# A gated recurrence in front of a routed expert layer: 29 instead of 24 warm-up products at the start of TensorE's queue

## The chip, the cores and the metric

The kernel runs on one core of one Trainium2 chip. The time is the device time of one execution in microseconds (us); the time of a kernel is the median of several executions. Lower is better.

## The reference

The first half is a recurrence over 768 tokens for 4 batches and 8 heads of width 48. Its output, 3072 rows of 384, goes to a layer of eight experts, where each row uses the one expert that its gate favours:

```python
f = 1.0 / (1.0 + np.exp(-f_logit))
for t in range(S):
    state = f[:, :, t, :, None] * state + np.einsum('bhd,bhe->bhde', k[:, :, t], v[:, :, t])
    y[:, :, t] = np.einsum('bhd,bhde->bhe', q[:, :, t], state)
x = y.transpose(0, 2, 1, 3).reshape(B * S, H * D)
expert_idx = np.argmax(x @ w_gate, axis=1)
# per expert e, on its rows:  relu(x @ w1[e]) @ w2[e], times the row's gate probability
```

Everything is in float32. The warm-up products that the change is about have no part in this result: they multiply a constant tile by itself into a buffer that the first real use starts afresh.

## The kernel before, in words

**Units.** The recurrence is cut into 12 units, each of 128 tokens for two batches. A unit has two halves, `a` and `b`. For each unit the forget gates are turned into running sums of logarithms (`exp`, `ln`, `sum`), the keys are scaled by the growth `r` (`kr`, or `krv` where VectorE does it), and the queries by the decay `dec` (`q`). TensorE then transposes the keys (`kp`, line 607), forms the scores of keys and queries (`sc`, line 594), applies them to the values (`wi`, line 618), adds what older states give (`bef`, line 639), and forms the addition to the state (`dp`, line 655). ScalarE copies the transposed keys out (`keep`, line 610), and VectorE masks the scores (`mx`, `my`, line 600).

**After the units.** The rows are projected to the gate and laid out (`xp`, line 717), and scattered into a buffer in memory that is sorted by expert (line 196). From about 117 us on, the experts' two products (lines 337 and 353, and 1117 and 1143 for short blocks) fill the rest of the time.

**The order of the work.** It is written out by hand. `FIRST_STEPS` is one list of steps for the first ten units, and each engine runs its share of the list in the order of the list; nothing reorders it afterwards. Every load of this stage is issued from SyncE's queue (SP), also in list order. So what stands in front of a TensorE step in this list also stands in front of it in TensorE's queue, and a step that TensorE can't start holds up all that stand behind it.

**The warm-up.** `fill24` calls `warm(24)`:

```python
for _ in range(count):
    nc.tensor.matmul(
        yt[0][:, 0], lhsT=pad[:, 0:C], rhs=pad[:, 0:C], start=True, stop=True
    )
```

(line 754). `pad` is a constant tile that GpSimd lays out at the start (lines 188 and 189); `yt` is cleared by VectorE (line 482). A float32 product takes two passes of the array, so 24 products are 48 instructions in the profile, each with its weight load. The first real TensorE step in the list is `kp0a`, the transposition of four blocks of unit 0's keys. It needs the scaled keys (`krv0a`, VectorE, line 560) and the identity matrix, which is loaded by the step `consts0` (line 165, `fpack<-c_fpack`). Behind it stands `sc0a`, which needs the scaled queries `q0a` (VectorE, line 583), then `fill8`, a second, shorter warm-up, then `kp0b`.

## Time and profile before

| what | value |
| --- | --- |
| time, median of 3 executions | 391.99 us (391.94 to 394.16) |
| the profiled execution's own time | 388.52 us |
| its span, first to last instruction | 386.5 us |
| what lies around the span | 2.02 us |
| TensorE busy | 377.2 us, 98% of the span, 3054 products |
| VectorE, ScalarE, GpSimd busy | 170.2, 102.3, 98.9 us |
| mean granted TensorE clock | 0.999 |
| mean DMA rate | 245 GB/s |

The profile is one execution. "Busy" of TensorE is the union of its instructions, which are pipelined: one starts before the one ahead of it has ended. So the distance from start to start, and not the length of one instruction, is what a product costs in a row of products. The profile also follows a chain back from the last instruction, at each step to what released it.

### The profile page before, as it was taken

To read this page: it belongs to the slowest core of one execution; us is meant where nothing else is said; L and a number is where in the kernel's file an instruction comes from. 1 tells how busy PE (TensorE), PEld (TensorE's weight loads), DVE (VectorE), ACT (ScalarE), POOL (GpSimd) and SP (SyncE) were. 2 spreads that over 40 slices of the span, in tenths; PEclk is the share of its full clock that TensorE was granted. 3 is DMA by queue.
4 is the path that set the end of the run, shared out by engine and by line. 5 is a ranking of instruction groups with operands and counts; after the bars stand their busy time and mean duration, and the time that the engine had idled before them with its cause. 6 is when DMAs were issued, how large, how long until landed. Compare 5 with 4: busy or idle time off the path is not lost.

```text
span 386.5 us, 7693 instructions
## 1 busy us (share of the span) xinstructions
PE 377.2 (98%) x3054; PEld 264.6 (68%) x3054; DVE 170.2 (44%) x367; ACT 102.3 (26%) x190; POOL 98.9 (26%) x120
## 2 busy tenths in 40 slices
PE   8899999999999999999999999999999999999993
PEld 8789988889989777685555555654466466455452
DVE  6899989897874632122121131116412113111360
ACT  6899885884532000010100110000010000001000
POOL 4444256658946310201002102100210210210112
PEclk9999999999999999999999999999999999999999
DMA  7999765759993559594649999898163369993141
GB/s 260 388 360 372 261 230 199 249 181 303 412 354 123 174 162 333 118 344 77 197 130 396 264 392 395 221 398 220 41 247 113 102 211 385 397 415 138 21 175 54
DMA packets 51659, 94.81 MB, mean 245 GB/s; under 512 B 20840, under 2 KB 40875, under 8 KB 49568
## 3 DMA queue, kind: packets, MB, share of 16 engines
q1 hardware_dynamic: 48448, 84.62, 64.5%
q0 software_dynamic: 3168, 9.64, 6.6%
q8 instruction: 25, 0.41, 0.4%
q14 instruction: 18, 0.15, 0.1%
HBM read 79.23 MB, written 15.21 MB: 244 GB/s over the span
## 4 chain that ended last, share of the span: by engine, by line
PE 85%; DMA 6%; issue 2%; POOL 2%; DVE 1%; SPq 1%; ACT 1%; POOLq 0%; ACTq 0%; DVEq 0%
PE hps L337 28%; PE yps L353 24%; PE yps L1143 7%; PE s L594 5%; PE yt L618 4%; PE xp L717 3%; DMA xs<-xr,posi 3%; PE s L337 3%; PE hps L1117 3%; PE yp L353 3%; PE kp L607 2%; DMA fpack<-c_fpack 2%; PE dp L655 2%; PE yt L639 1%; DMA xrow<-xs 1%
## 5 line engine op out<-in xcount | busy, mean ns | idle before, releaser
L337 PE MATMUL hps<-xT,w1t 128*128 128x352 f32 (+2 forms) x384 | 110.1, 447 | 0.0
L337 PEld LDWEIGHTS hps<-xT,w1t 128*128 128x128 f32 x384 | 72.7, 190 | 37.2 <-issue 1.9
L353 PE MATMUL yps<-w2t,hT 128*128 128x384 f32 x288 | 94.4, 487 | 0.0
L353 PEld LDWEIGHTS yps<-w2t,hT 128*128 128x128 f32 x288 | 54.6, 190 | 38.6 <-issue 1.5
L196 POOL DMA_INDIRECT out_dram<-ysb,dst x24 | 23.4, 974 | 224.7 <-DVE ysb L364 215.6
L347 ACT ACTIVATE hT<-hps 128x352 f32<-128x352 f32 (+2 forms) x28 | 13.7, 491 | 200.7 <-PE hps L337 200.7
L349 DVE TENSOR_SCALAR hT<-hps 128x352 f32<-128x352 f32 (+2 forms) x28 | 15.6, 558 | 93.0 <-PE hps L337 93.0
L364 DVE TENSOR_SCALAR ysb<-yps,tg 128x384 f32<-128x384 f32 x22 | 13.6, 618 | 74.4 <-PE yps L353 55.7
L600 DVE COPY_PREDICATED at<-mpack,s 128x512 f32<-128x512 uint8 x48 | 32.1, 732 | 3.1 <-PE s L594 3.1
L560 POOL TENSOR_TENSOR k<-k,r 128x1024 f32<-128x1024 f32 (+1 forms) x11 | 25.2, 2296 | 20.5 <-ACT r L556 14.6
L542 DVE TENSOR_TENSOR_SCAN sum<-g,cap 128x1032 f32<-128x1032 f32 (+1 forms) x14 | 28.2, 2022 | 2.2 <-ACT g L535 2.2
L196 POOL DMA_INDIRECT xs<-xr,posi x24 | 25.5, 1063 | 13.7 <-issue 4.6
L1143 PE MATMUL yps<-qw,hqT 128*32 128x192 f32 (+1 forms) x192 | 26.8, 380 | 0.0
L594 PE MATMUL s<-q,k 64*128 64x128 f32 x384 | 26.3, 281 | 0.1
L717 PE MATMUL xp<-wx,ys 128*128 128x104 f32 x192 | 24.9, 279 | 0.2 <-ACT ys L681 0.2
L594 PEld LDWEIGHTS s<-q,k 64*128 64x128 f32 x384 | 22.8, 187 | 2.6 <-issue 1.2
L618 PE MATMUL yt<-at,v 128*48 128x128 f32 x384 | 24.3, 276 | 0.0
L717 PEld LDWEIGHTS xp<-wx,ys 128*128 128x128 f32 x192 | 22.9, 192 | 1.0 <-ACT ys L681 0.3
L618 PEld LDWEIGHTS yt<-at,v 128*48 128x48 f32 x384 | 20.2, 123 | 2.1 <-issue 1.0
L1143 PE MATMUL yps<-w2t,hT 128*32 128x384 f32 x192 | 21.4, 487 | 0.0
L583 DVE TENSOR_TENSOR q<-q,g 128x1024 f32<-128x1024 f32 (+1 forms) x14 | 16.7, 1196 | 1.1 <-DMA q<-in_qu_dram 0.9
L1143 PEld LDWEIGHTS yps<-w2t,hT 128*32 128x32 f32 x192 | 7.6, 110 | 13.0 <-issue 12.5
(116 smaller groups left out, 354.9 us busy)
## 6 DMA issues: line engine op xcount, KB each, us to landing
qw<-in_moe_w_dram SPq DMA_DIRECT2D x16, 1536.0 KB, 12.9
w1t<-in_moe_w_dram SPq DMA_DIRECT2D x8, 1536.0 KB, 7.3
w2t<-in_moe_w_dram SPq DMA_DIRECT2D x8, 1536.0 KB, 15.8
k<-in_ku_dram SPq DMA_DIRECT2D x12, 512.0 KB, 6.1
q<-in_qu_dram SPq DMA_DIRECT2D x12, 512.0 KB, 6.2
f<-in_fu_dram SPq DMA_DIRECT2D x10, 512.0 KB, 6.3
xs<-pad SPq DMA_DIRECT2D x8, 600.0 KB, 3.9
v<-in_vu_dram SPq DMA_DIRECT2D x12, 384.0 KB, 5.1
```

Of the source, the lines that this page charges most:

```text
L196: ins = nc.gpsimd.indirect_dma_start(out=dst, out_offset=bass.IndirectOffsetOnAxis(ap=idx, axis=0), in_=src, in_offset=None, bounds_check= ...
L337: nc.tensor.matmul(x["h"][:, f], lhsT=w[0][:, j, b * 128 : b * 128 + 128], rhs=x["xT"][:, j], start=j == 0, stop=j == KD - 1,)
L349: nc.vector.tensor_scalar(to, x["h"], 0.0, None, op0=OP.max)
L353: nc.tensor.matmul(yp, lhsT=x["hT"][:, f, t * C : t * C + C], rhs=w[1][:, f, :], start=f == 0, stop=f == NF - 1,)
L542: nc.vector.tensor_tensor_scan(x["sum"][:, part].rearrange("p s c -> p (s c)"), x["g"][:, part].rearrange("p s c -> p (s c)"), cap[:, part ...
L560: ins = on.tensor_tensor(k, k, units[u]["r"][:, part], op=OP.mult).ins
L583: return nc.vector.tensor_tensor(q, q, x["dec"][:, part], op=OP.mult).ins
L594: done["score"] = nc.tensor.matmul(ps[h][:, p], lhsT=x["k"][r, s], rhs=x["q"][r, s], start=True, stop=True).ins
L600: nc.vector.copy_predicated(x["at"][:, a, h], _bc(causal, 1, HP), x["ps", a][h])
L618: nc.tensor.matmul(x["yt"][a][DP * (h ^ a) : DP * (h ^ a) + D, p], lhsT=x["v"][:, a, 2 * p + h], rhs=x["at"][:, a, h, p], start=p == 0, st ...
L717: nc.tensor.matmul(x["xp", a][:, p], lhsT=x["ys", a][:, p], rhs=wx[:, p, 0:XW] if a else wx[:, p, E:WX], start=True, stop=True,)
L1143: nc.tensor.matmul(yp[r], lhsT=h[:, f, at : at + T], rhs=w[:, f, cols], start=f == 0, stop=f == NF - 1, skip_group_check=True,)
```

## The change

The first warm-up has 29 products instead of 24. Nothing else differs: no load, no buffer, no wait and no order of the real steps.

```diff
     FIRST_STEPS = """
-        lf0a exp0a ln0a fill24 lf0b exp0b lk0 ln0b sum0a dec0a sum0b ends0 lf1a lq0 lf1b r0a
+        lf0a exp0a ln0a fill29 lf0b exp0b lk0 ln0b sum0a dec0a sum0b ends0 lf1a lq0 lf1b r0a
         r0b exp1a krv0a krv0b consts0 kp0a lk1 ln1a q0a sc0a lq1 exp1b ln1b dec0b keep0a
```

## The prediction

> **What bounds the kernel now.** I read the page's busy times first:

> ```profile
> PE 377.2 (98%) x3054; PEld 264.6 (68%) x3054; DVE 170.2 (44%) x367; ACT 102.3 (26%) x190; POOL 98.9 (26%) x120
> PEclk9999999999999999999999999999999999999999
> ```

> TensorE is the bound: 377.2 of 386.5 us, and its granted clock is full in every slice. Only 9.3 us of the span are not TensorE's, so I looked for where they lie. TensorE's waits answer that:

> ```profile
> PE yt L754 <- DVE yt L482: 1.6, 1, 1.6
> PE kp L607 <- DMA fpack<-c_fpack: 1.4, 1, 1.4
> PE xp L717 <- ACT ys L681: 0.2, 1, 0.2
> PE s L337 <- DVE xT L320: 0.2, 1, 0.2
> ```

> Four waits (us in total, times, longest), 3.4 us in all; the other 5.9 us are the tail behind the last product. The second wait is the one that the change sits in front of. Next the timeline of TensorE's first 16 us (start, length, line, count, idle time before it):

> ```profile
> 1.57 8.06 PE L754 MATMUL yt<-pad 128*128 128x128 f32 x48 [1.57 <-DVE yt L482]
> 11.03 0.63 PE L607 MATMUL kp<-fpack,k 128*128 128x128 f32 x4 [1.40 <-DMA fpack<-c_fpack]
> 11.58 1.16 PE L594 MATMUL s<-q,k 64*128 64x128 f32 x16
> 12.68 2.05 PE L754 MATMUL yt<-pad 128*128 128x128 f32 x16
> 14.56 0.60 PE L607 MATMUL kp<-fpack,k 128*128 128x128 f32 x4
> ```

> The 24 warm-up products end at 9.63. Then TensorE is idle for 1.40 us until the identity lands. The chain that ended last confirms who sets the start at 11.03:

> ```profile
> 3.56 7.33 DMA fpack<-c_fpack
> 10.89 0.14 issue
> 11.03 0.63 PE kp L607 x4
> 11.65 1.09 PE s L594 x16
> 12.75 1.98 PE yt L754 x16
> ```

> The chain runs through the load of the identity (issued 3.56, landed 10.89), not through the first warm-up. The second warm-up is on the chain, so from 11.03 on TensorE's queue has no slack: what delays `kp0a` delays what follows.

> Last, the pace of the warm-up, counted in equal stretches for line 754 (stretch, length, busy and count, granted clock, DMA share, GB/s):

> ```profile
> 4.00:6.00 2.00, 2.00 (x12) 1.00 0.83 287
> 7.00:9.00 2.00, 2.00 (x20) 1.00 1.05 391
> ```

> A count includes the two instructions or so that already run when a stretch begins, so some 9.5 start in the first 2 us and 18 in the second: 0.21 and 0.11 us each. Stretches that all begin at 1.50 and end 0.01 us apart give the single starts: 1.58, 1.92, then every 0.213 us up to 6.61, then from 6.79 every 0.111 us up to 9.36. So the array runs at half pace for 5.2 us (1.57 to 6.79) and at full pace after that. The granted clock reads 1.00 in both stretches; this halving has to be read from the starts.

> **The change part by part.** There is one edit: five more products.

> Count: five products are 10 passes (24 are 48), and 10 weight loads that run beside them. Duration: they are appended at the end of the row, where the pace is full, 10 x 0.111 = 1.11 us. The last pass would start at 9.36 + 1.11 = 10.47 and end at 10.74, and the next instruction could start at 10.47 + 0.11 = 10.58. `kp0a` cannot start before the identity is there, 10.89 + 0.14 = 11.03. So 0.45 us of cover is left, and the five products cost 0 in this execution. The work that hides them is the load of the identity. If that landed at once, `sc0a` just behind `kp0a` would still want `q0a`, whose multiplication on VectorE ends at 10.03 + 0.69 = 10.72; so a second cover lies 0.3 us below the first. With both gone the price is the whole 1.11 us.

> Upper end: the moment at which the pace doubles is not set by the program. If the doubling came later, the row would end later, and the appended passes could be slow ones. Each us of delay takes 1 - 0.111/0.213 = 0.48 us off the cover, so 0.45 us is used up when the doubling comes 0.94 us later, at 7.7. The far end is a row that never speeds up: 10 x 0.213 = 2.13 us. I take 0, since both covers are in the rows; 2.13 is kept for the range.

> Lower end, below nothing: the products can't bring `kp0a` forward, since it waits for a load that they don't touch. What they could save is pace behind the gap. With the five, the idle time shrinks from 1.40 to 0.29 us. If an idle time of 1.4 us, or a longer one, made the array fall back to half pace, the first real work would run slowly. What that would cost: regaining full pace took 5.2 us of steady work, in which 5.2 / 0.213 = 24 passes start; at full pace these take 24 x 0.111 = 2.7 us. A fall costs 2.5 us. The trace shows none: the four passes of `kp0a` start at 11.03, 11.17, 11.28 and 11.39, and the last 15 of the second warm-up's 16 every 0.11 us from 12.89 to 14.46. So the gain is 0 in this execution.

> What can move besides: SP's queue and GpSimd's have no instruction added or moved past, and no wait is added. VectorE, ScalarE and GpSimd don't wait for the first warm-up anywhere in the trace. TensorE's instruction stream grows by 20 of some 6,100, and the trace shows no TensorE idle time put down to the fetching of instructions: 0.

> [...]

> Sum: 0 against the profiled execution: span 386.5, with the 2.02 around it 388.52 us. The median of the unprofiled executions, 391.99, stands 3.47 us above that, and they reach from 391.94 to 394.16. One profile can't say what these 3.5 us are. Carrying 0 over to the median gives 392.0.

> **The rivals.**

> *B: the gap does cool the array in executions other than the profiled one, and 29 products prevent it.* For it: the 3.47 us between the profiled execution and the median would hold one fall (2.5 us), with 0.97 left over. If the rise came 1.7 us earlier than in the profile, at about 5.1, the 24 products would end 0.48 x 1.7 = 0.8 us earlier and the gap would be 2.2 us instead of 1.4; with 29 it would be 1.1. Against it: the 1.4 us gap left the pace alone. One fall saved gives 392.0 - 2.5 = 389.5; the whole 3.47 gives 388.5; two falls saved, 5.0 us, 387.0. It decides from the shortest gap that cools, which lies above 1.4 us if there is one.

> *C: the row overruns the load.* The place is the start of `kp0a`. It decides when the rise comes after 7.7 us, or when the identity and the queries are there before 10.58. For it: the cover is only 0.45 us, and nothing in TensorE's queue behind 11.03 would take up a delay before the 0.2 us waits at 112 and 117 us. Against it: the landing and the second cover would both have to be earlier, or the rise later by a fifth of its 5.2 us. The price is 0.2 us for a small overrun, 1.11 us with both covers gone, 2.13 us in a row that stays slow: 392.2 to 394.1. This is the case that ends slower than before.

> *D: the change does nothing that a measurement can tell.* That is the forecast itself, A, and its rival is only the spread of the executions: the four known ones lie between 388.52 and 394.16.

> **How the numbers follow.** A (hidden in the gap, with D's spread) 0.60; B 0.25; C 0.15. A is the likeliest, so 392.0 us is predicted. Its own range is that of the four known executions, 388.5 to 394.2, and more likely its upper part, where the three unprofiled ones lie. For 8 in 10 the range has to take in most of B and C: down to 388.2, just below B's 388.5, and up to 394.4, just above C's slow row and the highest execution. What is left out is B's two falls (0.10) and some 0.08 of spread on both sides.

> A measurement of this kernel can tell about 1% from no change, 3.9 us: below 388.1 is faster, above 395.9 slower. Faster: B's two falls 0.10, and 0.10 for B's 388.5 or A with the spread below it, 0.20. Slower: C's 394.1 needs 1.8 us of spread on top; 0.05 from C, 0.05 from A's spread, 0.10. Same: 0.70.

> **What would show each step right or wrong.** In the profile of the changed kernel the first row of line 754 should count 58, its starts should go from 0.213 to 0.111 us apart, and the wait of `kp` for `fpack` should shrink from 1.40 to about 0.3 us, while `kp0a` still starts at about 11.0. The span should be 386.5 within 1 us. C is right if `kp0a` has no wait in front and starts later than the landing plus 0.14. B can show only if unprofiled times fall to about 388.5 to 389.5 while the profiled execution stays as it was; a profile of the kernel with fewer warm-up products would then have to show 0.213 us between starts behind a longer gap. The forecast is wrong if the time moves by more than 1% either way, above all if it moves with an unchanged start of `kp0a` and an unchanged pace behind it: then something that I costed at nothing is not nothing.

## The result, and the profile after

The kernel with 29 products takes 392.23 us (median of 14 executions, 391.37 to 394.50), the one with 24 takes 392.00 us (14 executions, the three known ones among them, 390.97 to 394.16). The ratio is 1.0004, interval 0.9982 to 1.0025: no change that can be told, as forecast (392.0).

The profiled execution of the changed kernel took 392.63 us, with a span of 390.6 us. TensorE's timeline of the start (start, length, line, count, idle time before it):

```profile
1.57 8.18 PE L754 MATMUL yt<-pad 128*128 128x128 f32 x58 [1.57 <-DVE yt L482]
10.59 0.63 PE L607 MATMUL kp<-fpack,k 128*128 128x128 f32 x4 [0.84 <-DMA fpack<-c_fpack]
11.14 1.16 PE L594 MATMUL s<-q,k 64*128 64x128 f32 x16
12.24 2.05 PE L754 MATMUL yt<-pad 128*128 128x128 f32 x16
14.12 0.60 PE L607 MATMUL kp<-fpack,k 128*128 128x128 f32 x4
```

The first row counts 58 passes instead of 48, and TensorE still waits for the identity behind it, 0.84 us. The wait is not the 0.3 us that the working gave, because two things moved on their own. In the stretch counts of line 754 the pace doubled earlier (17 passes touch the stretch from 4 to 6 us, 12 before; read singly, the starts are 0.11 us apart from 4.68 on instead of 6.79):

```profile
4.00:6.00 2.00, 2.00 (x17) 1.00 0.85 284
7.00:9.00 2.00, 2.00 (x20) 1.00 1.03 338
```

And in the chain that ended last the load of the identity took 6.89 us instead of 7.33:

```profile
3.56 6.89 DMA fpack<-c_fpack
10.45 0.14 issue
10.59 0.63 PE kp L607 x4
```

So here the changed kernel was 0.44 us ahead at the transposition, for a reason that isn't the change, and yet its span is 4.1 us longer. TensorE's waits and its timeline show where most of that was lost:

```profile
PE yt L754 <- DVE yt L482: 1.6, 1, 1.6
PE yp L353 <- ACT hT L347: 1.5, 1, 1.5
PE kp L607 <- DMA fpack<-c_fpack: 0.8, 1, 0.8
```

Around 125 us, first in the kernel before, then in the changed one:

```profile
125.19 5.33 PE L353 MATMUL yp<-w2t,hT 128*128 128x384 f32 x16
```

```profile
125.34 0.91 PE L337 MATMUL s<-xT,w1t 128*128 128x128 f32 x6
127.78 6.98 PE L353 MATMUL yp<-w2t,hT 128*128 128x384 f32 x16 [1.52 <-ACT hT L347]
```

A wait of 1.5 us for ScalarE (line 347) stands in front of 16 passes that then take 6.98 us; in the kernel before the same 16 had no wait and took 5.33 us. The stretches around it (stretch, length, busy and count, granted clock, DMA share, GB/s) show why:

```profile
127.00:128.00 1.00, 0.22 (x1) 0.77 0.01 0
128.00:130.00 2.00, 2.00 (x4) 0.50 0.00 0
130.00:131.00 1.00, 1.00 (x3) 0.53 0.00 0
131.00:132.00 1.00, 1.00 (x4) 1.00 0.53 205
```

The granted clock fell to 0.50 at about 127.5 and came back at about 130.9. At half pace 3.4 us lose 1.7, and the 16 passes took 1.65 us longer. Another 1.3 us went between 90 and 125 us, part of it in waits of 0.2 to 0.3 us for which the profile names no releaser. Nothing suggests that this is the change's doing: none of the twelve profiles of the experiments below, two of them with 29 products, shows this wait or a fall at this place, and the ratio of the 14 to the 14 is 1.0004. But there is no profile of 24 products from the same set of executions, so it isn't shown that they have the wait too.

### The profile page after: what moved, and what is told of

The parts are those of the page before. It is cut to its first block, busy times and chain, and to the rows that moved or that the text cites. A ratio compares the mean times of both kernels' runs of the same rounds, so it can differ in the third digit from the quotient of the medians.

```text
span 390.6 us, 7713 instructions
## 1 busy us (share of the span) xinstructions
PE 380.0 (97%) x3064; PEld 266.1 (68%) x3064; DVE 170.5 (44%) x367; ACT 102.6 (26%) x190; POOL 99.9 (26%) x120
## 4 chain that ended last, share of the span: by engine, by line
PE 95%; DMA 2%; DVE 1%; SPq 1%; issue 0%; POOL 0%; ACT 0%; POOLq 0%
PE hps L337 28%; PE yps L353 24%; PE yps L1143 7%; PE s L594 7%; PE xp L717 6%; PE yt L618 6%; PE yp L353 3%; PE s L337 3%; PE hps L1117 3%; PE yt L639 3%; PE kp L607 3%; PE dp L655 2%; DMA fpack<-c_fpack 2%; SPq L517 1%; PE yt L754 1%
## 5 line engine op out<-in xcount | busy, mean ns | idle before, releaser
L337 PE MATMUL hps<-xT,w1t 128*128 128x352 f32 (+2 forms) x384 | 110.1, 447 | 0.0
L337 PEld LDWEIGHTS hps<-xT,w1t 128*128 128x128 f32 x384 | 72.7, 190 | 37.2 <-issue 1.9
L196 POOL DMA_INDIRECT xs<-xr,posi x24 | 27.3, 1138 | 16.3 <-issue 4.9
L542 DVE TENSOR_TENSOR_SCAN sum<-g,cap 128x1032 f32<-128x1032 f32 (+1 forms) x14 | 29.2, 2093 | 2.0 <-ACT g L535 1.9
L594 PE MATMUL s<-q,k 64*128 64x128 f32 x384 | 26.7, 282 | 0.1
L717 PE MATMUL xp<-wx,ys 128*128 128x104 f32 x192 | 24.9, 279 | 0.4 <-issue 0.4
L594 PEld LDWEIGHTS s<-q,k 64*128 64x128 f32 x384 | 23.1, 187 | 2.7 <-issue 1.2
L717 PEld LDWEIGHTS xp<-wx,ys 128*128 128x128 f32 x192 | 22.9, 192 | 1.2 <-issue 0.9
L583 DVE TENSOR_TENSOR q<-q,g 128x1024 f32<-128x1024 f32 (+1 forms) x14 | 15.6, 1121 | 1.0 <-DMA q<-in_qu_dram 0.8
```

The lines of the kernel that those rows point to most:

```text
L196: ins = nc.gpsimd.indirect_dma_start(out=dst, out_offset=bass.IndirectOffsetOnAxis(ap=idx, axis=0), in_=src, in_offset=None, bounds_check= ...
L337: nc.tensor.matmul(x["h"][:, f], lhsT=w[0][:, j, b * 128 : b * 128 + 128], rhs=x["xT"][:, j], start=j == 0, stop=j == KD - 1,)
L542: nc.vector.tensor_tensor_scan(x["sum"][:, part].rearrange("p s c -> p (s c)"), x["g"][:, part].rearrange("p s c -> p (s c)"), cap[:, part ...
L583: return nc.vector.tensor_tensor(q, q, x["dec"][:, part], op=OP.mult).ins
L594: done["score"] = nc.tensor.matmul(ps[h][:, p], lhsT=x["k"][r, s], rhs=x["q"][r, s], start=True, stop=True).ins
L717: nc.tensor.matmul(x["xp", a][:, p], lhsT=x["ys", a][:, p], rhs=wx[:, p, 0:XW] if a else wx[:, p, E:WX], start=True, stop=True,)
```

## The experiments

Each experiment ran on a chip with its own executions of the kernel with 24 products, and a ratio is against those. The median of 24 products was 388.42 us on the first chip of the experiments (runs 1 to 4), 387.71 on the second (5 to 8) and 387.81 on the third (9 to 12), against 392.00 where the result was taken. These sets differ by up to 4.3 us with nothing changed, more than any of the rivals but the largest end of B; whether it is the chip or the occasion that differs was not separated. The expectations of runs 1 to 4 were worked out from 392.0, so their times in us miss by this difference, and only the ratios can be compared. Where a run is called so many us slower, that is its ratio applied to the median of 24 products.

Two numbers recur below. The copy of GpSimd at line 171 waits for the same load of the identity. It shows when that landed, even where TensorE's row is longer: where `kp` waited too, the copy started 0.01 to 0.02 us ahead of it. And an execution's mean granted clock: the two profiles with a fall in the middle of the work, the result's and run 3's, have 0.991 and 0.993, the twelve others 0.995 to 0.999, some of them lowered by a fall behind TensorE's last product, which cost nothing. So an execution at 0.994 or less is taken to have had a fall somewhere in the middle.

**1. The unchanged kernel again.** No edit.

> The unchanged kernel with 24 products, once more, as the yardstick for one profile against another. Cover theory (the row of products is hidden under the load of the identity): the row of 48 passes ends between 8.6 and 10.4 us, the transposition starts 0.14 us after the load's landing, near 10.6 to 11.0, and the time is 392.0 within 1. If the first profile's 388.5 was the rule and the later times the exception, the span would be 386.5 again; if it was a lucky execution, the span is 389 to 392, as the changed kernel's was, and the TensorE wait for the ScalarE copy near 126 us and the fall of the granted clock behind it turn up here too, with no change made. Cooling theory (the longer gap of 24 products makes the array fall back to half pace): 0.213 us between starts behind the gap, and 2.5 us lost there.

388.25 us (12 executions, 386.88 to 390.48); ratio 0.9999, interval 0.9973 to 1.0026; profiled span 385.4 us. The gap is as in the first profile:

```profile
10.05 0.63 PE L607 MATMUL kp<-fpack,k 128*128 128x128 f32 x4 [1.43 <-DMA fpack<-c_fpack]
```

The row ended at 8.62 and the transposition started at 10.05, half a microsecond earlier than expected, because the identity landed earlier. There are no 0.213 us distances behind the gap and no wait near 126 us. So the first profile's 388.52 was no lucky execution for such a chip; it fits these times and not the 392. Over this experiment and its yardstick, 13 of 41 executions have a mean clock of 0.994 or less, and those take 2 us more than the others (medians 389.7 to 390.1 against 387.8). The kernel with 24 products does lose something in some executions; where, the profile doesn't show, since this execution has no fall.

**2. No first warm-up.**

```diff
-        lf0a exp0a ln0a fill24 lf0b exp0b lk0 ln0b sum0a dec0a sum0b ends0 lf1a lq0 lf1b r0a
+        lf0a exp0a ln0a lf0b exp0b lk0 ln0b sum0a dec0a sum0b ends0 lf1a lq0 lf1b r0a
```

> The first warm-up is left out altogether (24 to 0 products). Cover theory: the array has never risen when the transposition starts at 10.6 to 11.0 us, so the real work and the second warm-up run at 0.213 us between starts until the pace doubles 3 to 5.2 us later; that costs 1.6 to 2.5 us, time 393.6 to 394.5, ratio 1.004 to 1.006. Rival (the pace of the early part does not matter, since other engines set its end): the start is slow but the time stays at 392.0, ratio 1.000. Rival (the row does harm): below 391.

390.99 us, ratio 1.0048, interval 1.0026 to 1.0070: 1.9 us slower, as the cover theory had it. TensorE's timeline begins with real work at half pace:

```profile
10.79 1.09 PE L607 MATMUL kp<-fpack,k 128*128 128x128 f32 x4 [10.79 <-DMA fpack<-c_fpack]
11.81 2.08 PE L594 MATMUL s<-q,k 64*128 64x128 f32 x16
13.82 3.11 PE L754 MATMUL yt<-pad 128*128 128x128 f32 x16
16.77 0.60 PE L607 MATMUL kp<-fpack,k 128*128 128x128 f32 x4
```

From `kp0a` to `kp0b` it is 5.98 us instead of 3.53; the single starts are 0.21 us apart until 16.1. The pace of the early work does reach the end, so the warm-up earns its place: it must have raised the pace by the time that the real work starts.

The clocks of the 12 executions say more than the text of this run asked for. None is at 0.994 or less, against 13 of 41 with 24 products on the same chip. Without the row no clock has risen that the gap could take back; a fall at some later place would not go away with the row.

**3. 12 products.** The edit is `fill12` in the same place.

> 12 instead of 24 products: the row of 24 passes ends near 6.8 us and leaves a gap of some 4 us before the transposition. Cooling theory: a gap of 4 us lets the array fall back, or never lets it rise, and the real work starts at 0.213 us; 1.6 to 2.5 us lost, as with no row at all, ratio 1.004 to 1.006. If even a gap of 4 us leaves the pace alone, starts behind the gap are 0.111 us apart and the time is 392.0; then neither the 1.4 us gap of 24 nor the shorter one of 29 can matter.

390.83 us, ratio 1.0050, interval 1.0026 to 1.0073. The pace had doubled at 6.3 us, and the gap took it back:

```profile
1.57 5.12 PE L754 MATMUL yt<-pad 128*128 128x128 f32 x24 [1.57 <-DVE yt L482]
9.73 1.09 PE L607 MATMUL kp<-fpack,k 128*128 128x128 f32 x4 [3.04 <-DMA fpack<-c_fpack]
10.77 2.08 PE L594 MATMUL s<-q,k 64*128 64x128 f32 x16
```

Here the granted clock shows the fall too (before the first rise of an execution it reads 1.00, though the starts are 0.213 us apart; stretch, length, busy and count, granted clock, DMA share, GB/s):

```profile
9.00:9.50 0.50, 0.00 (x0) 1.00 1.09 438
9.50:10.00 0.50, 0.27 (x2) 0.60 1.01 410
10.00:12.50 2.50, 2.50 (x20) 0.50 1.02 412
12.50:13.00 0.50, 0.50 (x5) 0.50 1.01 397
13.00:13.50 0.50, 0.50 (x5) 0.99 1.09 426
```

It fell at 9.6 and came back at 13.0. All 12 executions have a mean clock of 0.994 or less. Here the clock fell within a gap of 3.04 us, and the row of 12 was worth nothing: the time is that of no row at all.

**4. 64 products.** The edit is `fill64`.

> 64 products: 80 passes more than with 24, at 0.111 us each 8.9 us. Cover theory: 0.45 to 2.1 us of it lie in the gap (the landing of the load and the moment of the rise both vary), the rest delays everything behind one for one: 6.8 to 8.4 us more, 398.8 to 400.4, ratio 1.017 to 1.021, with no wait for the load left in front of the transposition. Rival (the early part of TensorE's queue has slack that takes a delay up, since the loads bound that stage): less than half of it arrives at the end, below 396.

396.16 us, ratio 1.0184, interval 1.0151 to 1.0216: 7.1 us slower. The chain that ended last now runs through the warm-up and no longer through the load:

```profile
0.94 0.50 DVE yt L482
1.44 0.14 issue
1.57 17.47 PE yt L754 x128
19.04 0.44 PE kp L607 x4
```

The identity had landed by 10.56 (GpSimd's copy), the transposition started at 18.88. What overruns the load, 8.3 us in this execution, whose pace doubled late, at 7.8, arrives at the end nearly one for one (7.1 us by the ratio). There is no gap here that could cool, and none of the 6 executions has a clock of 0.994 or less.

**5. 29 products, on the second chip.** No edit to the changed kernel.

> The changed kernel (29 products) beside the unchanged one on the same chip, with the mean granted clock of each execution. On the chip of the first four experiments the executions of the kernel with 24 products fell in two groups: about 45 in 100 had a mean clock of 0.995 or less and took about 2 us longer than the others at 0.996 or more. Cover theory, with the fall of the clock somewhere behind the first 20 us: 29 products change neither group nor their shares; ratio 1.000. Cooling theory (in the slower executions the gap in front of the transposition cooled the array, and five more products prevent it): hardly any execution at 0.995 or less, and a median lower by about 1 us, ratio 0.997.

388.18 us (387.62 to 389.13), ratio 1.0011, interval 0.9991 to 1.0032. The row just met the load: the copy of GpSimd starts at 9.82, the transposition at 9.83, with no wait in front that the profile shows. None of 12 executions has a clock of 0.994 or less, but on this chip only 1 of 29 with 24 products has one either, so the shares decide nothing here.

**6. 18 products.** The edit is `fill18`.

> 18 products: 12 passes fewer than 24, so the row ends 1.3 us earlier (2.6 us if the pace has not doubled by then) and the gap in front of the transposition is 2.4 to 3 us, between the 1.4 us that left the pace alone and the 3.0 us behind which 12 products were found at half pace. If only a gap near 3 us and above cools: 0.111 us between starts behind the gap and ratio 1.000 to 1.002. If 2.4 us is enough: 0.213 us between starts, 1.6 to 2.5 us lost, ratio 1.004 to 1.006 as with 12.

389.02 us (6 executions), ratio 1.0040, interval 1.0027 to 1.0052: as slow as with 12. But the profiled execution kept its pace behind a longer gap than that of 24:

```profile
10.41 0.63 PE L607 MATMUL kp<-fpack,k 128*128 128x128 f32 x4 [2.33 <-DMA fpack<-c_fpack]
10.97 1.16 PE L594 MATMUL s<-q,k 64*128 64x128 f32 x16
```

It was the shortest of the six (388.01 us). One of the six has a clock of 0.994 or less. The other five are without such a clock, and yet their median stands 1.4 us above that of the executions of 24 products without one (389.02 against 387.65), so a fall doesn't account for this loss; what does was not found. Run 11 repeats it.

**7. 34 products.** The edit is `fill34`.

> 34 products: 20 passes more than 24, 2.2 us at 0.111 us. Cover theory: 0.45 to 1.6 us of cover, so 0.6 to 1.8 us arrive at the end, ratio 1.0015 to 1.0045, and no wait for the load in front of the transposition, or almost none. Slack theory: ratio 1.000, as with 29.

389.18 us, ratio 1.0046, interval 1.0025 to 1.0067: 1.8 us slower, at the upper end of what was expected. GpSimd's copy starts at 10.37, the transposition at 10.82, and the chain of waits has the row in place of the load:

```profile
1.57 9.42 PE yt L754 x68
10.99 0.44 PE kp L607 x4
```

This execution's pace doubled early, at 4.9, and it overran by 0.45 us; a rise at 6.8 would make that an estimated 1.4 us (0.48 us for each us, as worked out in the prediction).

**8. Four more products near 126 us.** The first warm-up stays at 24.

```diff
                 widen(soon[0], weights[0], early_h, range(7, NF))
+                warm(4)
                 turn(soon[1])
```

> 24 products as before, and 4 more (8 passes, 0.89 us) in front of the first product that waits for ScalarE near 126 us, where the changed kernel's profile showed an idle 1.5 us and the granted clock falling to half behind it. If the slower executions come from a fall at that place: the share of executions with a mean clock of 0.995 or less goes from about 45 in 100 to under 15, those cost up to 0.9 us less, and the others 0.9 us more; ratio 0.999 to 1.002. If they come from the gap at 10 us: the share stays, and all executions take 0.9 us longer, ratio 1.002.

388.85 us, ratio 1.0027, interval 1.0012 to 1.0043: 1.0 us slower, about the plain price of 8 passes (0.89 us). On this chip the unchanged kernel had hardly any fall to prevent (1 of 29), so whether products at that place would help on a chip with more of them stays open.

**9. and 12. The unchanged kernel, two more profiles.** No edit.

> The unchanged kernel a third time, for its spread and for another profile. In the profiles so far gaps of 1.4 to 1.7 us and of 2.6 us in front of the transposition left the pace at 0.111 us, and one of 3.3 us did not. Cover theory: 0.111 us behind the gap again, and where an execution has a fall of the granted clock at all, it lies far behind 20 us. Cooling theory: a profile of 24 products whose clock has fallen shows the fall at 9 to 13 us.

> The unchanged kernel, one more profile. Cover theory: full pace behind the gap and, where the clock falls, a fall behind 20 us; cooling theory: the fall at 9 to 13 us.

387.52 us, ratio 0.9992, interval 0.9971 to 1.0013, and 387.52 us for the single execution of run 12. The gaps were 1.04 and 1.44 us, with 0.11 us between starts behind both, and neither execution has a fall before its tail. No profile of 24 products caught one, so the place of the falls that their clocks tell of was not seen.

**10. 29 products, on the third chip.** No edit to the changed kernel.

> 29 products once more beside 24, for the interval. Cover theory: ratio 0.999 to 1.002, the upper part where the load lands early: on the second chip it landed in time for a start at 9.83 us, which leaves the row of 29 no cover, so that up to 0.4 us of it shows. Cooling theory: ratio below 0.998.

388.03 us (387.26 to 389.31), ratio 0.9998, interval 0.9983 to 1.0013. Here the row did overrun. Its pace doubled at 7.4, and the chain runs through it:

```profile
1.57 9.45 PE yt L754 x58
11.02 0.44 PE kp L607 x4
```

The copy of GpSimd starts at 10.71, the transposition at 10.86: 0.15 us late.

**11. 18 products again.**

> 18 products once more, since six executions were 0.4% above the kernel with 24 although the profiled one kept its pace behind the gap of 2.6 us. If a gap of 2.6 us cools in some executions and not in others: the ratio stays at 1.003 to 1.005, and about half of the executions have a mean clock of 0.995 or less; if this profile shows the fall, it lies at 10 to 14 us. If the six were a poor sample: ratio 1.000 to 1.002.

388.92 us (12 executions), ratio 1.0024, interval 1.0004 to 1.0045. Five of 12 executions have a clock of 0.994 or less; their median is 390.0, that of the others 388.2. The profiled one had a gap of 1.61 us and kept its pace. So a part of the executions with 18 products have a fall, and only a part. (The 2.6 us in the expectation are counted from the last start of the row to the transposition; the idle time in run 6 was 2.33 us.)

## Why the prediction was right, point by point

**The signs.** The first row did count 58 and went from 0.213 to 0.111 us between starts. The other signs that the prediction named for its case did not come: the wait was 0.84 us and not about 0.3, the start 10.59 and not about 11.0, the span 390.6 and not 386.5 within 1. The first two moved with the rise and the landing, the third with what happened from 90 to 131 us. The forecast of 392.0 held because the 0 was carried over to the median, and the two medians are of one set of executions.

**The price of a pass** (one of the two instructions that the profile shows for a product; 0.111 us from start to start at full pace, 0.213 at half) held in every profile. Before the first rise of an execution only the starts show which of the two it is; the granted clock there reads 1.00.

**The cover** held as a kind and was too precise as a size. The working had 0.45 us left behind 29 products, from one landing and one rise. Over the 14 profiles the identity let GpSimd start between 9.72 and 11.02 us, and in the 13 with a first row the pace doubled between 4.7 and 7.8. In the result's profile the transposition stood 0.84 us behind the row of 29; in run 5 it stood at the row's end; in run 10 it was 0.15 us late, and with 34 products 0.45 us late. So 29 is not "hidden with 0.45 to spare" but about at the edge: A in one execution and C in the next. Among executions with a clock above 0.994, 29 products stand 0.5 us above 24 on the second chip (388.18 against 387.65) and 0.3 us on the third (388.03 against 387.77). C's mechanism exists, at about the 0.2 us that it was given for a small overrun.

**The second cover**, the queries behind the identity, was not tried by itself. In 13 of the 14 profiles, among them the early landing of run 5, `q0a` ended 0.3 to 0.4 us ahead of the GpSimd copy that waits for the identity (at 10.72 against 11.02 in the first profile, at 10.27 against 10.58 in the result's): it moved with the first cover. The case in which it would count, that the identity alone comes early, was seen once, in run 3 (`q0a` ended at 10.72, the copy started at 9.72).

**The loss by a fall** was mis-sized: 2.5 us, taken from the 5.2 us that the first rise took. The fall lasted 3.4 us in both profiles that show one (9.6 to 13.0 and 127.5 to 130.9), which at half pace is 1.7 us lost; behind 127.5 the 16 passes took 1.65 us longer.

**B, that the gap cools the array in some executions**, was given 0.25, and its mechanism turned out partly true. Executions with a mean clock of 0.994 or less, each chip by itself:

| first row | first chip | second chip | third chip |
| --- | --- | --- | --- |
| none | 0 of 12 | | |
| 12 products | 12 of 12 | | |
| 18 products | | 1 of 6 | 5 of 12 |
| 24 products | 13 of 41 | 1 of 29 (run 8: 1 of 12) | 6 of 41 |
| 29 products | | 0 of 12 | 0 of 12 |
| 34 products | | 0 of 12 | |
| 64 products | 0 of 6 | | |

(The limit is rough: two executions with 34 products had 0.995 and took 391.9 and 392.1 us, 3 us above the others.) In the rows of 12 products and more, a shorter one came with no fewer such executions in the hundred, on each chip, and in the profiles of runs 3, 6 and 1 with a longer gap (3.04, 2.33 and 1.43 us). On the first chip that is clear of chance: where there is no gap behind a risen clock (no row, 64 products) none of 18 executions has such a clock, against 13 of 41 with 24 products. On the second and third the single steps are not clear of chance. The place of the fall is seen for 12 products alone; for 18 and 24 it is inferred from these shares, and no profile caught it. Where the result was taken 7 of 14 executions with 29 products had a clock that low, one of them by the wait near 126 us; the place in the other six, and the share with 24 products there, are not on record. On the third chip the executions with such a clock take 1.7 to 2.5 us more than the others, and 6 of 41 of them come to 0.3 us in the mean, about what 29 products cost there by the overrun.

So the sum of 0 left out two terms of a few tenths. On the third chip five more products came with fewer falls and with an overrun, of about the same size and opposite sign; on the second there was hardly a fall to take away. Both terms are below what the spread of 3 us lets a median show. That they about cancel is luck; where the result was taken neither is shown, and the one profile has the row hidden. B's large ends, 389.5 and less, needed a fall at the gap in the median execution; the ratios of 24 against 29 (1.0004, 1.0011 and 0.9998) show no such gain.

**The 3.47 us between the first profile and the first median**, which the prediction left open and B wanted to use, are of the size by which the sets of runs differ: 24 products take 387.7 to 388.4 on the three chips of the experiments, which the first profile's 388.52 fits. What differs there was not found. The wait near 126 us is one place, in one profile, and falls are not enough: the seven executions with 29 products that have a clock above 0.994 still take 391.6 us (median).

**The gap and the pace.** At the start, gaps of 0.84 to 2.33 us left the pace in every profile that had one, one of 3.04 us didn't. At 127.53 us the clock fell within an idle time of 1.52 us. So a length of gap that left the pace alone at 10 us was not safe there.

## What to carry to other kernels

A row of warm-up products was free here up to the landing of what the first real product waits for, and cost nearly its full pace behind that (with 64 products 7.1 us of an overrun of 8.3); the bottom lies at 24 to 29 products, with 0.2 to 0.5% to lose on either side (18 and 34, the loss at 18 only in part explained). Both ends of such a gap moved by more than a microsecond between executions (the start that the identity allowed from 9.72 to 11.02 us, the doubling of the pace from 4.7 to 7.8, an estimated 1.5 us at the row's end), so work out the cover for the early and the late landing and the early and the late rise, not for the one that the profile happens to show. And before a profile is laid beside a median, ask whether the two come from the same chip and the same set of executions: the same kernel's medians here lie up to 4.3 us apart.

## What the runs showed of the hardware that was not expected

How busy TensorE was in the 3.413 us in front of such a time (by the profile's lengths of the instructions, counted in stretches from the rise) went with whether the clock stayed. Six stretches were busy for 15 to 38% of the time, and each ended in a fall: 15% with 12 products, and in the stretch in which the last product ended 38% in the result's profile and, estimated from the stretch counts and their mean clocks, 17, 38, 29 and 24% in runs 8 to 11. Of a stretch with 52% (378.80 to 382.21 us in the kernel before), one with 58% (run 1, below) and one with 56% (124.12 to 127.53 us in the changed kernel's profile) only the last did. Idle time alone doesn't sort them: 1.52 us idle in front of 127.78 came with the fall, 2.33 us in front of the transposition in run 6 did not.

How the same kernel could cool in one execution and not in the next can only be estimated. In run 1, with 24 products and the rise at 4.62 us, the whole gap lay within one stretch (8.04 to 11.45 us), which was 58% busy, and the clock stayed. Had the identity let the transposition start at 11.03 us as in the first profile, the same stretch would have been busy for some 30%, an estimate from these two profiles (0.58 us in front of the gap and 0.42 behind it), and each of the six stretches with 15 to 38% ended in a fall. Five more products, 1.11 us, would have made it some 62%. No profile shows this case itself.
